# Issuing the scatters of three sequences one at a time between the steps of a recurrent stage (attention, routed experts and a dense block on one Trainium2 core)

## Chip, cores and metric

The kernel runs on one core of one Trainium2 chip. The metric is the device time of one execution in microseconds (us). Three runs of the kernel before gave 576.25, 574.99 and 574.95 us, so its time is the median, 574.99 us.

## What is computed

Three parts follow one another. A gated linear recurrence over 4 sequences (b) of 768 tokens with 8 heads gives 3072 rows of 384 values. A router then sends part of the rows to one of 8 experts each, and a dense block with a maximum over three products makes the output.

```python
for t in range(S):                                    # recurrence, per b and head
    state = alpha[:, :, t, :, None] * state + einsum('bhd,bhe->bhde', k[:, :, t], v[:, :, t])
    y[:, :, t] = einsum('bhd,bhde->bhe', q[:, :, t], state)
...
do_compute = x @ w_skip > 0                           # routed experts
e_idx = argmax(xc @ w_gate)
y[mask] = gate_w[mask, None] * (maximum(xc[mask] @ w1[e], 0.0) @ w2[e])
out[do_compute] = xc + y
...
h = maximum(maximum(x @ w1, x @ w2), x @ w3)          # dense block
return h @ w_out
```

## The kernel before

**Chunks.** The recurrence is cut into 24 chunks of 128 tokens, 6 for each sequence; chunk n = 6b + c is the n-th turn of the loop `for n, (b, c) in enumerate(seq)`. In turn n TensorE (PE) does, in this order: `scores(n+1)` (L284, keys by queries), `trans(n+1)` (L275), `rows(n-1)` (L330, the output of the chunk before, turned to token rows), `outs(n)` (L317 with the running state, L320 with the masked scores), and `upd(n)` (L302, the state's update). In this document chunk n begins where the first L320 product of chunk n starts.

**Around PE.** VectorE (DVE) makes two scans for chunk n+3 (L241, L255), two masks of the scores of chunk n+1 (L290), and adds the old state to the new (L305, reads PE's L302). ScalarE (ACT) copies out of the accumulators: `yt` (L323, reads PE's L317 and L320 and feeds L330), the rows `xr` (L349), and the scaled state `ws` (L307, reads DVE's L305 and feeds L317 of the next chunk). GpSimd (POOL) multiplies the keys and the queries by the scans' results: `k` at L244 and `q` at L259, one each a chunk, for chunk n+3; PE needs them two turns later.

**Router and scatters.** When the six chunks of a sequence are through, its 768 rows are given slots. For sequences 0 and 1 the generator `early` does this, for sequences 2 and 3 the generator `route` (sequence 3 in two parts of 4 and 2 chunks). A generator yields between its steps, and `step_routes()`, called twice a turn (after `outs` and at the turn's end), takes it one step on. `route` finds the expert of each row (`om`, L460), counts (`ec`, L462), asks PE for the ranks in two small products (`pr`, L471 and L472, which read `om` and `ec`), and works out the slot numbers `si` (L476 to L485). Then POOL scatters the rows: six indirect DMAs a sequence (L415), each of 128 rows of 386 values (384 values, a weight, the token's number) to the table `slots` in DRAM. In `scatter` the pace is set by yields:

```python
if b == B - 2 and 0 < c < NC - 1:      # sequence 2: one scatter a step
    yield 1
elif b < B - 2 and c % 2 and c < NC - 1:   # sequences 0, 1: two, then one turn on
    yield 1
    yield 1
```

POOL itself takes its queue in order and starts a scatter as soon as `si` and the rows are there. After turn 20 there are no more `k` and `q` to make, so nothing stands between the six scatters of sequence 2 in POOL's queue.

**After the chunks.** In turn 22 the queue of SP loads the first 256 rows of `slots` back (`xe`, L619), which waits for the scatters of sequences 0 to 2; PE reads `xe` at L642 after chunk 23. The six scatters of sequence 3 come after that. Then the experts begin (first product at L756), and from there PE is busy to the end.

Of the kernel before, what the change touches and what calls it, by code (L numbers as in the profile page):

```python
# [83 lines left out]
def tile_gla_moe_moe2(ctx, tc, akq, vp, wgt, cst, io, ew, md, out):  # L84
# [41 lines left out]
    with tc.manual_schedule():  # L126
# [135 lines left out]
        def prep(j):  # L262
            if j < nseq:
                sf = suffixes(j)
                inverse(j, sf)
                prefixes(j, sf)
# [88 lines left out]
            return low_part  # L355

        nroute = [0]
        scat = []
        ecs = []

        def early(b, c0, c1):
            om = wk.tile([128, NE, NC + 1], BF16, name=f"om{NC}")
            ec = wk.tile([128, NE, NC + 1], BF16, name=f"ec{NC}")
            r = lambda nm, w, dt=F32: wk.tile([128, NC, w], dt, name=nm)
            mx, md, sm, ra, s1, dl, rk = (r(*z) for z in (
                ("mx", 1), ("md", 1), ("sme", 1), ("ra", 1), ("s1", 1), ("dl", NE), ("rk", NE)))
            s2, mi = (cols[nm][:, 0:NC, None] for nm in ("s2", "mi"))
            t = cols["t"].rearrange("p (c e) -> p c e", c=NC)
            si, lh, ls_, tr_ = r("si", 1, I32), r("lh", 18), r("lgs", NE + 1), r("tr", 6)
            ex, xb, l8 = exs[b % 2], xr[b], ls_[:, :, 0:NE]  # L370
            bc = lambda a: a.to_broadcast([128, NC, NE])
            ce = lambda a: a.rearrange("p e c -> p c e")
            fl = lambda a: a.rearrange("p e c -> p (e c)")
            h = lx[b].rearrange("p c a e -> p c (a e)")
            nroute[0] += 1
            A.copy(om[:, :, 0:1], ecs[-1] if ecs else cnt[:, :, None])
            G.tensor_tensor(lh, h[:, :, 0:18], h[:, :, 18:36], ALU.add)
            G.tensor_tensor(ls_, lh[:, :, 0:9], lh[:, :, 9:18], ALU.add)
            SY.dma_start(out=x2[b * S:(b + 1) * S, :].rearrange("(c p) d -> p c d", p=128), in_=xb[:, :, 0:DM])
            yield 1  # L380
            V.tensor_reduce(mx, l8, AX.X, ALU.max)
            G.tensor_tensor(dl, l8, bc(mx), ALU.subtract)
            yield 1
            yield 1
            V.scalar_tensor_tensor(t, dl, 0.0, cols["rev"][:, None, :].to_broadcast([128, NC, NE]), ALU.is_equal, ALU.mult)
            V.tensor_reduce(mi, t, AX.X, ALU.max)
            V.scalar_tensor_tensor(md, ls_[:, :, NE:NE + 1], 0.0, mi, ALU.is_le, ALU.add)
            A.activation(ex[:, :, 0:NE], dl, AF.Exp)
            yield 1
            V.tensor_tensor(ce(om)[:, 1:], t, bc(md), ALU.is_equal)  # L390
            V.tensor_tensor_scan(fl(ec), cols[NC].bitcast(BF16), fl(om), 0.0, ALU.mult, ALU.add)
            ecs.append(ec[:, :, NC:NC + 1])
            yield 1
            pr = ps_r.tile([128, NE, NC], F32, name="pr")
            T.matmul(pr, ltri, om[:, :, 1:], start=True, stop=False)
            T.matmul(pr, ones, ec[:, :, 0:NC], start=False, stop=True)
            G.tensor_tensor(tr_[:, :, 0:4], ex[:, :, 0:4], ex[:, :, 4:8], ALU.add)
            G.tensor_tensor(tr_[:, :, 4:6], tr_[:, :, 0:2], tr_[:, :, 2:4], ALU.add)
            G.tensor_tensor(sm, tr_[:, :, 4:5], tr_[:, :, 5:6], ALU.add)
            G.tensor_tensor(sm, sm, ex[:, :, NE:], ALU.add)  # L400
            yield 1
            V.tensor_tensor(rk, ce(pr), ce(om)[:, 1:], ALU.mult)
            V.tensor_reduce(ra, rk, AX.X, ALU.add)
            V.scalar_tensor_tensor(s1, mi, -float(CAP), ra, ALU.mult, ALU.add)
            A.copy(xb[:, :, DM + 1:DM + 2], tokid[:, b * NC:(b + 1) * NC, None])
            yield 1
            V.reciprocal(xb[:, :, DM:DM + 1], sm)
            V.tensor_scalar(s2, ra, float(CAP - OFF), 8192.0, ALU.is_ge, ALU.mult)
            V.scalar_tensor_tensor(si, s2, float(OFF + NSLOT), s1, ALU.add, ALU.add)
            yield 1  # L410
            yield from scatter(b, 0, NC, si)

        def scatter(b, c0, c1, si):
            for c in range(c0, c1):
                i_ = G.indirect_dma_start(  # L415
                    out=slots, out_offset=bass.IndirectOffsetOnAxis(ap=si[:, c - c0, :].bitcast(U32), axis=0),
                    in_=xr[b][:, c, :], in_offset=None, bounds_check=NSLOT - 1, oob_is_err=False)
                for j_ in scat:
                    tc.declare_no_dep(i_.ins, j_.ins, reason="every row of every scatter has a slot of its own")
                scat.append(i_)  # L420
                if b == B - 2 and 0 < c < NC - 1:
                    yield 1
                elif b < B - 2 and c % 2 and c < NC - 1:
                    yield 1
                    yield 1
            yield 1

        def route(b, c0, c1):
            n = c1 - c0
# [36 lines left out]
                         in_=xb[:, :, 0:DM])  # L466
            yield 1
            if not last:
                yield 1
            pr = ps_r.tile([128, NE, n], F32, name="pr")  # L470
            T.matmul(pr, ltri, om[:, :, 1:], start=True, stop=False)  # L471
            T.matmul(pr, ones, ec[:, :, 0:n], start=False, stop=True)  # L472
# [13 lines left out]
            def onehot():  # L486
                for c in range(n):
                    V.tensor_scalar(p0[:, c0 + c], iota[:, 0:CAP], s2[:, c], None, ALU.is_equal)
                    yield 1 if c0 + c == 0 else 0
                yield 1  # L490

            if last:
                if c0:
                    A.copy(cnt, ec[:, :, n])
                yield from onehot()
                V.tensor_scalar(si[:, 0:n], s2, 0.0, None, ALU.add)
            V.tensor_reduce(sm, ex, AX.X, ALU.add)
            V.reciprocal(xb[:, :, DM:DM + 1], sm)
            A.copy(xb[:, :, DM + 1:DM + 2], tokid[:, b * NC + c0:b * NC + c1, None])
            yield from scatter(b, c0, c1, si)  # L500

        rw, wr = {}, {}

# [35 lines left out]
        def step_routes():  # L539
            for r in reversed(routes):  # L540
                stage(r)
# [19 lines left out]
        for n, (b, c) in enumerate(seq):  # L561
            if n + 1 < nseq:
                scores(n + 1)
                trans(n + 1)
            if n < 2:
                prep(n + 2)
            elif n == 2:
                prefixes(4, half)
            else:
                prep(n + 3)  # L570
            if n + 1 < nseq:
                mask(n + 1, 0)
                mask(n + 1, 1)
            if n == 1:
                half = first_half(4)
            if n == 2:
                prep(5)
            low_part = rows(n - 1) if n else None
            if n == nseq - 2:
                A.copy(xq[0][:, 0:2], xr[B - 1][:, 0:2, 0:DM])  # L580
                rA = route(B - 1, 0, 4)
            if n > nseq - 3:
                stage(rA)
            outs(n)
            step_routes()
            upd(n)
            if n > nseq - 3:
                stage(rA)
            if n == nseq - 1:
                xlow(0)  # L590
            if n > nseq - 4:
                low_part()
            if n == 0:
                vload(4)
            vload(n + 5)
            if n and seq[n - 1][1] == NC - 1:
                routes.append((early if b < B - 1 else route)(b - 1, 0, NC))
            step_routes()
            if n == 3:
                V.tensor_copy(cols["rev"], rev)  # L600
            if n == 10:
                SY.dma_start(out=iota, in_=io)
            if 3 <= n < 7:
                for i in range((n - 3) * NSLOT // 512, (n - 2) * NSLOT // 512):
                    SY.dma_start(out=slots[i * 128:(i + 1) * 128, :], in_=zt)
            if 7 <= n < 11:
                wpart(n - 7)
            if n in (13, 14, 15, 19):
                wsplit(min(n - 13, 3), G)
            if n in (17, 20):  # L610
                wload((n - 14) // 3)
            if n == nseq - 4:
                rs.close()
                xep = xes.enter_context(tc.tile_pool(name="xep", bufs=1, side="right"))
                xq += [xep.tile([128, NC, DM], F32R, name=f"xq{i}") for i in range(2)]
                p0 = xep.tile([128, NC, CAP], F32R, name="p0")
                xe = xep.tile([128, 2, DM], F32, name="xe")
            if n == nseq - 2:
                SY.dma_start(out=xe, in_=slots[0:CAP, 0:DM].rearrange("(m p) d -> p m d", p=128))  # L619
# [848 lines left out]
```

## Time and profile before

| | before |
|---|---|
| median of three runs | 574.99 us |
| the profiled execution: its own time | 575.13 us |
| the profiled execution: span from first to last instruction | 573.3 us |
| PE busy in the span | 562.1 us (98%) |
| DVE, ACT, POOL busy in the span | 408.8, 300.5, 257.7 us |
| granted clock of PE, mean over the span | 0.994 |
| scatters at L415 | 24, busy 23.7 us |

The profiled execution's own time is 1.8 us above its span, which is the work around the program, and 0.14 us above the median of the runs. The page gives busy time by engine and by slice of the span; the timelines give each instruction's start, length, and the time that its engine sat idle before it, with what ended the wait. A busy share is a mean over stages with different limits: what an edit of the scatters is worth stands in the stretch of the chunks (about the first 140 us) and in the waits there.

### The profile page before, as it was taken

Reading aid. Unit: us, or ns where it says so; the run is one execution under the profiler, and the core shown is the slowest. Engines: PE = TensorE matmul, PEld = TensorE weight load, DVE = VectorE, ACT = ScalarE, POOL = GpSimd, SP = SyncE. Lnnn points to the kernel's source line nnn. Section 1 sums busy time; section 2 is a strip of 40 time slices with the busy share of each in tenths; the row PEclk is TensorE's granted clock in tenths of the full one; section 3 lists DMA queues with packets and bytes.
Section 4 is the critical chain, followed back from the end, with each engine's and each line's share of the span. In section 5 each row is a group of like instructions: output and inputs, shape, how many; then the busy total and the mean of one; then the engine's idle time right before and its main releaser. Section 6 shows DMA issues by size and latency. Waiting matters only on the chain. (4 is left out here: it accounts for less than half of the span.)

```text
span 573.3 us, 11006 instructions
## 1 busy us (share of the span) xinstructions
PE 562.1 (98%) x4149; PEld 502.8 (88%) x4149; DVE 408.8 (71%) x697; ACT 300.5 (52%) x654; POOL 257.7 (45%) x216
## 2 busy tenths in 40 slices
PE   7999999979999999999999999999999999999997
PEld 4999888969999999999988888888788899787896
DVE  8998979927677767777589995694667584766700
ACT  4666676634667676667343445454544474455311
POOL 6654789843366555756222022112554501456320
PEclk9999999979999999999999999999999999999999
DMA  8899997743668988895328159335654624556011
GB/s 324 315 297 337 377 363 247 279 154 141 208 245 306 319 308 293 269 306 207 116 100 284 37 186 365 137 125 177 219 196 151 223 96 145 186 195 217 2 57 59
DMA packets 51150, 122.79 MB, mean 214 GB/s; under 512 B 4594, under 2 KB 38752, under 8 KB 47504
## 3 DMA queue, kind: packets, MB, share of 16 engines
q1 hardware_dynamic: 47856, 116.19, 58.7%
q0 software_dynamic: 2560, 4.83, 2.2%
q10 hardware_dynamic: 672, 0.98, 0.6%
q8 instruction: 34, 0.56, 0.4%
q14 instruction: 28, 0.23, 0.1%
HBM read 92.76 MB, written 32.28 MB: 218 GB/s over the span
## 5 line engine op out<-in xcount | busy, mean ns | idle before, releaser
L124 POOL TENSOR_TENSOR wl<-raw,wh 128x768 fp32r<-128x768 f32 x26 | 53.7, 2064 | 32.8 <-ACT wh L123 31.9
L123 ACT CAST wh<-raw 128x768 fp32r<-128x768 f32 x64 | 53.5, 837 | 14.6 <-PE po L776 13.9
L756 PE MATMUL ph<-xh,wh 128*128 128x256 f32 x192 | 56.4, 294 | 0.0
L757 PE MATMUL ph<-xl,wh 128*128 128x256 f32 x192 | 54.4, 283 | 0.1
L758 PE MATMUL ph<-xh,wl 128*128 128x256 f32 x192 | 54.4, 283 | 0.0
L776 PE MATMUL po<-wh,hl 128*128 128x384 f32 x128 | 43.2, 337 | 0.0
L775 PE MATMUL po<-wl,hh 128*128 128x384 f32 x128 | 43.1, 337 | 0.0
L774 PE MATMUL po<-wh,hh 128*128 128x384 f32 x128 | 42.9, 335 | 0.0
L124 DVE TENSOR_TENSOR wl<-raw,wh 128x768 fp32r<-128x768 f32 x38 | 36.4, 958 | 9.0 <-ACT wh L123 8.4
L762 DVE SCALAR_TENSOR_TENSOR hl<-ph,hh 128x256 fp32r<-128x256 f32 x64 | 26.8, 419 | 16.5 <-ACT hh L761 15.2
L244 POOL TENSOR_TENSOR k<-akq,sf 128x512 f32<-128x512 f32 x24 | 28.4, 1185 | 19.7 <-DVE sf L241 12.3
L757 PEld LDWEIGHTS ph<-xl,wh 128*128 128x128 f32 x192 | 36.4, 190 | 0.5 <-issue 0.3
L756 PEld LDWEIGHTS ph<-xh,wh 128*128 128x128 f32 x192 | 36.5, 190 | 0.2 <-ACT xh L123 0.2
L758 PEld LDWEIGHTS ph<-xh,wl 128*128 128x128 f32 x192 | 36.3, 189 | 0.0
L415 POOL DMA_INDIRECT slots<-xr,si x24 | 23.7, 987 | 23.8 <-DVE s L482 15.5
L761 ACT ACTIVATE hh<-ph 128x256 fp32r<-128x256 f32 x64 | 24.7, 385 | 16.2 <-PE ph L758 12.7
L284 PE MATMUL ps<-q,k 64*128 64x128 f32 x384 | 30.0, 286 | 2.2 <-POOL q L259 1.8
L255 DVE TENSOR_TENSOR_SCAN ap<-akq,pcs 128x521 f32<-128x521 f32 x24 | 29.8, 1241 | 1.8
L259 POOL TENSOR_TENSOR q<-akq,ap 128x512 f32<-128x512 f32 x24 | 28.4, 1183 | 5.6 <-DVE ap L255 5.6
L241 DVE TENSOR_TENSOR_SCAN sf<-akq,pcs 128x520 f32<-128x520 f32 x24 | 29.5, 1228 | 1.5 <-DMA akq<-in_akq_dram 1.3
L290 DVE TENSOR_TENSOR sm<-ps,cs 128x512 f32<-128x512 f32 x48 | 30.3, 673 | 0.0
L1141 POOL TENSOR_TENSOR tb<-tb,tb 128x512 f32<-128x512 f32 x12 | 15.5, 1293 | 31.5 <-ACT tb L1140 31.5
(683 smaller groups left out, 1734.2 us busy)
## 6 DMA issues: line engine op xcount, KB each, us to landing
raw<-in_ew_dram SPq DMA_DIRECT2D x15, 1536.0 KB
akq<-in_akq_dram SPq DMA_DIRECT2D x21, 772.5 KB
rm<-in_md_dram SPq DMA_DIRECT2D x12, 768.0 KB
mh<-wd SPq DMA_DIRECT2D x7, 1024.0 KB
ml<-wd SPq DMA_DIRECT2D x7, 896.0 KB
raw<-wd SPq DMA_DIRECT2D x6, 1024.0 KB
raw<-wd SPq DMA_DIRECT2D x6, 896.0 KB
vt<-in_vp_dram SPq DMA_DIRECT2D x24, 200.0 KB
```

The costliest lines, as they stand in the source:

```text
L123: A.copy(h, src)
L124: (eng or V).tensor_tensor(l, src, h.bitcast(F32), ALU.subtract)
L241: V.tensor_tensor_scan(sf[:, KW - 2::-1], al[:, KW - 1:0:-1], eb[:, KW - 1:0:-1], 0.0, ALU.mult, ALU.max)
L255: V.tensor_tensor_scan(ap, al, eb, 0.0, ALU.mult, ALU.max)
L284: T.matmul(ps[i][:, p, :], kh[j][r0:r0 + 64, p, :], qh[j][r0:r0 + 64, p, :], start=True, stop=True)
L290: V.tensor_tensor(t, fr[j][i], cmask[:, None, :].to_broadcast([128, NP, C]), ALU.mult)
L756: T.matmul(ph, wh[:, z], xh_[e][:, k, :], start=(k == 0), stop=False)
L757: T.matmul(ph, wh[:, z], xl_[e][:, k, :], start=False, stop=False)
L758: T.matmul(ph, wl[:, z], xh_[e][:, k, :], start=False, stop=(k == k3 - 1))
L774: T.matmul(po, hh[:, zm], wh, start=(f == 0), stop=False)
L775: T.matmul(po, hh[:, zm], wl, start=False, stop=False)
L776: T.matmul(po, hl[:, zm], wh, start=False, stop=(f == nf1 - 1))
```

## The change

The pace of the scatters is no longer set by yields in `scatter`. `early` and `route` put their six scatters into a list (`pend_sc`), and `scatter_next()` takes one from it at fixed places: in turns 3 to 19 between `k` and `q` of chunk n+3 and at the turn's end; in turn 20 after `k` and at the end; from turn 21 on after `rows(n-1)` and at the end. For sequence 2 the scatters of chunks 2 to 5 each follow a copy of the token's numbers on ACT (`late`), which POOL has to wait for; the copy stood before as one for all six chunks. To have `si` earlier, `route` of sequence 2 also takes its steps sooner: the weight (L497, L498) moves ahead, the ranks `pr` go to PE at the end of turn 19 and no longer within turn 20, and the slot numbers are made ahead of the masks in turn 20. Sequence 3 is scattered as before.

```diff
--- before.py
+++ after.py
@@ -408,22 +408,23 @@
             V.scalar_tensor_tensor(si, s2, float(OFF + NSLOT), s1, ALU.add, ALU.add)
             yield 1
-            yield from scatter(b, 0, NC, si)
-
-        def scatter(b, c0, c1, si):
-            for c in range(c0, c1):
...
-                if b == B - 2 and 0 < c < NC - 1:
-                    yield 1
-                elif b < B - 2 and c % 2 and c < NC - 1:
-                    yield 1
-                    yield 1
+            pend_sc.extend((b, c, si, False) for c in range(NC))
             yield 1
+
+        def scatter(b, c, si, late):
+            if late:
+                A.copy(xr[b][:, c, DM + 1:DM + 2], tokid[:, b * NC + c:b * NC + c + 1])
+            i_ = G.indirect_dma_start(
...
+        def scatter_next():
+            if pend_sc:
+                b, c, si, late = pend_sc.pop(0)
+                scatter(b, c, si[:, c, :], late)
@@ -466,7 +467,9 @@
             yield 1
             if not last:
-                yield 1
+                V.tensor_reduce(sm, ex, AX.X, ALU.add)
+                V.reciprocal(xb[:, :, DM:DM + 1], sm)
+                A.copy(xb[:, 0:2, DM + 1:DM + 2], tokid[:, b * NC:b * NC + 2, None])
             pr = ps_r.tile([128, NE, n], F32, name="pr")
@@ -489,15 +492,20 @@
-            if last:
-                if c0:
-                    A.copy(cnt, ec[:, :, n])
...
+            if not last:
+                pend_sc.extend((b, c, si, c > 1) for c in range(NC))
+                yield 1
+                return
...
-            yield from scatter(b, c0, c1, si)
+            for c in range(n):
+                scatter(b, c0 + c, si[:, c, :], False)
+            yield 1
@@ -566,16 +574,28 @@
-            else:
-                prep(n + 3)
+            elif n + 3 < nseq:
+                half = suffixes(n + 3)
+                if n + 4 < nseq:
+                    scatter_next()
+                inverse(n + 3, half)
+                if n + 4 < nseq:
+                    prefixes(n + 3, half)
+                else:
+                    step_routes()
+                    scatter_next()
             if n + 1 < nseq:
                 mask(n + 1, 0)
                 mask(n + 1, 1)
+            if n + 4 == nseq:
+                prefixes(n + 3, half)
...
             low_part = rows(n - 1) if n else None
+            if n + 3 >= nseq:
+                scatter_next()
@@ -596,6 +616,7 @@
             step_routes()
+            scatter_next()
```

On POOL the six scatters of sequence 1 and of sequence 2 stand as follows (`xr_818` is the row tile of sequence 1, `xr_1309` of sequence 2, `xr_1801` of sequence 3); before:

```order
L415 DMA slots_64<-xr_818,si_1256 2048x386 x2
L244 TENSOR_TENSOR k2_1697<-akq1_170,sf_1694 128x512
L259 TENSOR_TENSOR q2_1704<-akq1_170,ap_1700 128x512
L415 DMA slots_64<-xr_818,si_1256 2048x386 x2
L244 TENSOR_TENSOR k2_1783<-akq2_171,sf_1780 128x512
L259 TENSOR_TENSOR q2_1790<-akq2_171,ap_1786 128x512
L124 TENSOR_TENSOR wl_1841<-raw_859,wh_1840 128x768
L244 TENSOR_TENSOR k2_1864<-akq3_172,sf_1861 128x512
L259 TENSOR_TENSOR q2_1871<-akq3_172,ap_1867 128x512
L415 DMA slots_64<-xr_1309,si_1926 2048x386 x6
L415 DMA slots_64<-xr_1801,si_2135 2048x386 x4
```

and with the change:

```order
L417 DMA slots_64<-xr_818,si_1256 2048x386
L259 TENSOR_TENSOR q2_1704<-akq1_170,ap_1700 128x512
L417 DMA slots_64<-xr_818,si_1256 2048x386
L244 TENSOR_TENSOR k2_1780<-akq2_171,sf_1777 128x512
L417 DMA slots_64<-xr_818,si_1256 2048x386
L259 TENSOR_TENSOR q2_1790<-akq2_171,ap_1786 128x512
L124 TENSOR_TENSOR wl_1847<-raw_859,wh_1846 128x768
L244 TENSOR_TENSOR k2_1870<-akq3_172,sf_1867 128x512
L417 DMA slots_64<-xr_1309,si_1879 2048x386
L259 TENSOR_TENSOR q2_1892<-akq3_172,ap_1888 128x512
L417 DMA slots_64<-xr_1309,si_1879 2048x386 x5
L417 DMA slots_64<-xr_1801,si_2139 2048x386 x4
```

The scatters of sequence 1 stand alternately with `k` and `q` where they stood in pairs; of sequence 2 one stands ahead of the last `q`, and the other five follow it with nothing between them on POOL's own queue.

On ACT the copies of the token's numbers (`xr<-cs`) that the scatters of sequence 2 wait for stand so in turns 20 to 22; before:

```order
L307 ACTIVATE ws_139<-pu,totm 128x48 x4
L499 COPY xr<-cs 128x6
L277 COPY kk<-pk 128x512
L348 CAST xq_1945<-px 128x384
L349 COPY xr<-px 128x384
L323 COPY yt<-py 128x512
L307 ACTIVATE ws_138<-pu,totm 128x48 x4
```

and with the change:

```order
L307 ACTIVATE ws_139<-pu,totm 128x48 x4
L277 COPY kk<-pk 128x512
L348 CAST xq_1945<-px 128x384
L349 COPY xr<-px 128x384
L416 COPY xr<-cs 128x1
L323 COPY yt<-py 128x512
L307 ACTIVATE ws_138<-pu,totm 128x48 x4
L416 COPY xr<-cs 128x1
```

One copy for six chunks has become one copy ahead of each of four scatters (two of the four stand in these rows), half a turn apart; a copy for the first two chunks stands earlier, in turn 19.

On PE the ranks of sequence 2 (`pr`; `om` and `ec` come from DVE) stand in turn 20 before:

```order
L320 MATMUL py<-sm_1794,vt 64x128
L471 LDWEIGHTS ltri
L471 MATMUL pr<-om_1748,ltri 128x48
L472 LDWEIGHTS ones
L472 MATMUL pr<-ec_1749,ones 128x48
L302 MATMUL pu<-vt,kk 64x48 x8
```

and with the change at the end of turn 19:

```order
L320 MATMUL py<-sm_1708,vt 64x128
L302 MATMUL pu<-vt,kk 64x48 x8
L474 LDWEIGHTS ltri
L474 MATMUL pr<-om_1748,ltri 128x48
L475 LDWEIGHTS ones
L475 MATMUL pr<-ec_1749,ones 128x48
L284 MATMUL ps_1850<-q_1704,k_1694 128x128
```

They stood between L320 and L302 of chunk 20; now the scores of the next chunk stand right behind them in PE's queue.

## Rows read from the trace of the kernel before

**Rows 1.** Stretches, one chunk each, and three others: length, busy time, clock, DMA.
```profile
core 0: us, PE busy (x) PEld busy (x) DVE busy (x) ACT busy (x) POOL busy (x), PEclk, DMA share, GB/s
51.41:56.46 5.05, 5.05 (x79) 4.60 (x77) 4.57 (x11) 3.46 (x13) 2.10 (x2) 1.00 1.08 342
...
56.46:61.42 4.96, 4.96 (x76) 4.29 (x74) 4.11 (x10) 2.49 (x11) 2.82 (x6) 1.00 1.02 310
...
105.06:110.28 5.22, 5.22 (x78) 4.78 (x76) 5.01 (x11) 3.53 (x10) 4.29 (x5) 1.00 0.82 307
110.28:115.64 5.36, 5.36 (x80) 4.70 (x78) 4.04 (x14) 3.65 (x12) 4.09 (x4) 1.00 0.67 230
115.64:126.16 10.52, 6.77 (x74) 5.44 (x72) 2.91 (x9) 3.06 (x11) 4.93 (x6) 0.85 0.26 98
126.16:131.46 5.30, 5.30 (x61) 5.00 (x59) 2.48 (x13) 2.33 (x9) 0.00 (x0) 0.65 0.71 223
...
139.80:145.00 5.20, 5.13 (x38) 4.93 (x38) 2.46 (x5) 1.92 (x6) 3.89 (x5) 1.00 0.30 107
...
124.30:129.70 5.40, 5.40 (x52) 4.98 (x52) 2.75 (x11) 2.82 (x10) 0.00 (x0) 0.50 0.63 191
```

**Rows 2.** POOL's timeline: start, length (us), line, operation, idle before and its end.
```profile
105.44 0.97 POOL L415 DMA_INDIRECT slots<-xr,si  x1 [0.30 <-issue]
...
112.29 1.17 POOL L259 TENSOR_TENSOR q<-akq,ap 128x512 f32<-128x512 f32 x1
114.72 1.01 POOL L415 DMA_INDIRECT slots<-xr,si  x1 [1.26 <-issue]
...
121.13 0.97 POOL L415 DMA_INDIRECT slots<-xr,si  x1 [0.30 <-issue]
```

**Rows 3.** PE's timeline, the products of chunks 19 to 22 and L642.
```profile
105.06 1.10 PE L320 MATMUL py<-sm,vt 128*64 128x128 f32 x16
...
106.54 1.34 PE L284 MATMUL ps<-q,k 64*128 64x128 f32 x16
...
110.28 1.09 PE L320 MATMUL py<-sm,vt 128*64 128x128 f32 x16
...
115.64 1.09 PE L320 MATMUL py<-sm,vt 128*64 128x128 f32 x16
116.57 0.62 PE L302 MATMUL pu<-vt,kk 128*64 128x48 f32 x16
...
124.26 1.97 PE L317 MATMUL py<-q,ws 64*64 64x128 f32 x16 [2.18 <-ACT ws L307]
126.16 1.97 PE L320 MATMUL py<-sm,vt 128*64 128x128 f32 x16
...
136.50 0.69 PE L642 MATMUL pk<-cs,xe 128*128 128x128 f32 x4
```

**Rows 4.** ACT's timeline, the copies out of chunks 19, 20, 21, and the state.
```profile
107.03 0.59 ACT L323 COPY yt<-py 128x512 f32<-128x512 f32 x1 [1.61 <-PE pu L302]
...
111.42 0.59 ACT L323 COPY yt<-py 128x512 f32<-128x512 f32 x1 [0.47 <-PE py L320]
...
118.96 0.59 ACT L323 COPY yt<-py 128x512 f32<-128x512 f32 x1 [3.30 <-PE ps L284]
123.72 0.88 ACT L307 ACTIVATE ws<-pu,totm 128x48 f32<-128x48 f32 x4 [4.17 <-DVE pu L305]
```

**Rows 5.** DVE's timeline, the counts of sequence 2 and the state of chunk 21.
```profile
107.13 0.27 DVE L462 TENSOR_TENSOR_SCAN ec<-pcs,om 128x56 bf16<-128x56 bf16 x1
...
123.31 0.37 DVE L305 TENSOR_TENSOR pu<-pu,ws 128x192 f32<-128x192 f32 x1 [7.42 <-PE px L330]
```

**Rows 6.** Sum over the five stretches 61.42:66.87, 75.49:80.88, 91.07:96.30, 99.88:105.06, 105.06:110.28.
```profile
sum 26.47, PE 26.42 PEld 23.87 DVE 23.31 ACT 17.44 POOL 22.22; mean PE 5.28 PEld 4.77 DVE 4.66 ACT 3.49 POOL 4.44
```

**Rows 7.** SP's queue, the load of xe.
```profile
125.85 0.45 SPq L619 DMA_DIRECT2D xe<-slots  x1
```

**Rows 8.** The line view of L415: shortest, median, longest in ns, first and last start.
```profile
L415 POOL DMA_INDIRECT slots<-xr,si x24: 967/970/1164, 64.5 to 143.9; - x24
```

More of the change, by code (lines that the diff above doesn't have):

```diff
@@ L357, in tile_gla_moe_moe2 @@
         nroute = [0]
-        scat = []
+        scat, pend_sc = [], []
         ecs = []
@@ L410, in early @@
             yield 1
-            yield from scatter(b, 0, NC, si)
-        def scatter(b, c0, c1, si):
-            for c in range(c0, c1):
[L415 to L420, printed above, removed]
-                if b == B - 2 and 0 < c < NC - 1:
-                    yield 1
-                elif b < B - 2 and c % 2 and c < NC - 1:
-                    yield 1
-                    yield 1
-            yield 1
+            pend_sc.extend((b, c, si, False) for c in range(NC))
+            yield 1
+        def scatter(b, c, si, late):
+            if late:
+                A.copy(xr[b][:, c, DM + 1:DM + 2], tokid[:, b * NC + c:b * NC + c + 1])
+            i_ = G.indirect_dma_start(
+                out=slots, out_offset=bass.IndirectOffsetOnAxis(ap=si.bitcast(U32), axis=0),
+                in_=xr[b][:, c, :], in_offset=None, bounds_check=NSLOT - 1, oob_is_err=False)
+            for j_ in scat:
+                tc.declare_no_dep(i_.ins, j_.ins, reason="every row of every scatter has a slot of its own")
+            scat.append(i_)
+        def scatter_next():
+            if pend_sc:
+                b, c, si, late = pend_sc.pop(0)
+                scatter(b, c, si[:, c, :], late)
         def route(b, c0, c1):
@@ L490, in onehot @@
                 yield 1
-            if last:
-                if c0:
-                    A.copy(cnt, ec[:, :, n])
-                yield from onehot()
-                V.tensor_scalar(si[:, 0:n], s2, 0.0, None, ALU.add)
+            if not last:
+                pend_sc.extend((b, c, si, c > 1) for c in range(NC))
+                yield 1
+                return
+            if c0:
+                A.copy(cnt, ec[:, :, n])
+            yield from onehot()
+            V.tensor_scalar(si[:, 0:n], s2, 0.0, None, ALU.add)
             V.tensor_reduce(sm, ex, AX.X, ALU.add)
```

## Prediction

> **What bounds the kernel now.** The page comes first: PE is busy in 98% of the span, so a gain can lie only where PE idles, is held up, or runs at a lower clock. The stretches are next, cut where the L320 products of a chunk start [rows 1]. A chunk without scatters takes 5.05 us with PE busy throughout, and 4.96 us where the next chunk needs no transpose: this is PE's own pace. One chunk falls out: chunk 21 takes 10.52 us with PE busy for 6.77 of them, and chunk 22 takes 5.30 us at a mean granted clock of 0.65. In the middle of that, from 124.30 to 129.70 us, the granted clock is 0.50, the 1.2 GHz level; PE had been mostly waiting for the 6 us before.
>
> What sits in that hole is read from POOL's timeline [rows 2]: six scatters of sequence 2, one after another without a break, from 114.72 to 122.10 us (the first and the last stand in the rows, 0.30 us between neighbours). PE's timeline [rows 3] shows that L302 of chunk 21 was over at 116.57 + 0.62 = 117.19 us, and DVE's that the addition which reads it started at 123.31 us, after 7.42 us of idling [rows 5]; the scaled state came at 123.72 [rows 4] and L317 of chunk 22 only at 124.26 us [rows 3]. So DVE had its operands, had nothing else to do, and still waited until 1.2 us after the last scatter. The copy `yt` measures this three times [rows 4] against the end of the L320 products that it waits for [rows 3]: with no scatter about (chunk 20) it starts 111.42 − 111.37 = 0.05 us after them, beside a pair of scatters (chunk 19; the second runs to 106.41 [rows 2]) 107.03 − 106.16 = 0.87 us, beside the six 118.96 − 116.73 = 2.23 us. I read this so: while scatters are issued, word from one engine to another comes late, and in an unbroken run of them it piles up. That is an inference from three waits, not something a row states.
>
> **The change part by part.** Durations are those of the profiled execution, so the sum starts from its 575.13 us (0.14 above the median of the runs).
>
> *The run of six is broken up.* The change makes five of the six wait for something on ACT or DVE, or for their place behind `q`. One goes ahead of the last `q`, one behind it, four behind copies half a turn apart on ACT, so some 2 us apart on average, and words can pass between them. Chunk 21 then falls back to PE's pace, 10.52 − 4.96 = **5.56 us** gained; chunk 20 loses its surplus, 5.36 − 5.05 = **0.31 us**. Chunk 22 gets the full clock: its L320 products take 1.97 us at half clock against 1.09 us [rows 3], 0.88 us on the path, and half of the L330 products behind them adds some 0.2: **1.1 us**.
>
> *The ranks go to PE a turn earlier.* They now stand ahead of the scores of chunk 21, which started at 106.54 us [rows 3], and wait for `ec`, which ends at 107.13 + 0.27 = 107.40 us [rows 5]. PE has nothing to put in the gap, so it loses 0.86 us and about 0.1 for the start; if the last scatter of sequence 1, which now stands behind `k` and so beside this very wait, delays it by the 0.87 us seen beside a pair, 1.8 us. I take **−1.3 us**, between. The products themselves cost the same in either place.
>
> *Six single scatters beside chunks 20 to 23.* Not shown before. Low end nothing; far end what the run costs, 5.56 us, which is a rival below. The nearest rows are the five chunks with pairs, 26.47 us in sum [rows 6], so 26.47 − 5 × 5.05 = 1.2 us for five pairs, 0.24 us a pair. These chunks have less work to hide a late word behind than the earlier ones, so I take most of a pair's price for each single: **−1.2 us** (0 to −2.4).
>
> *Twelve single scatters of sequences 0 and 1.* Their number, length and order among `k` and `q` stay; `q` has the same work ahead of it and `k` one scatter less. Best, the 1.2 us of the pairs vanish; worst, each single costs 0.24, which is 12 × 0.24 − 1.2 = 1.7 us lost. I take **+0.6 us**.
>
> *DVE and ACT.* Weight and slot numbers move ahead of the last scan and the masks in turn 20. The masks of chunk 21 come some 1 us later; their scores are ready at 106.54 + 1.34 = 107.88 us and the L320 products that read them start at 115.64 us [rows 3], time enough for both. The last `q` ended at 112.29 + 1.17 = 113.46 us [rows 2] for scores that follow L302 at 117.19; with one scatter (0.97) and the later scan ahead of it, it ends some 1.5 us later and still in time. Four small copies on ACT replace one: they sit beside ACT's idling (it is busy for 3.06 of 10.52 us in chunk 21 [rows 1]). Without that cover each would cost less than the 0.59 us of a `yt` copy [rows 4].
>
> *The load of xe.* It waits for the last scatter of sequence 2, whose copy now stands behind the state of chunk 22. From the end of L302 of that chunk (T): the addition 0.37 [rows 5], the state 0.88 [rows 4], copy and starts, so a scatter at T + 1.9; in the trace the load was issued 125.85 − 121.13 = 4.7 us after the last scatter's start [rows 7, 2], part of it behind another store, so I put it at 2.5 to 4.7 later. Its 0.39 MB at the 223 GB/s of that stretch [rows 1] take 1.8 us: ready at T + 6.2 to 8.4. PE wants it at 136.50 us, 8.4 us after the L320 products of chunk 22 end [rows 3]; less 0.62 for L302 and some 0.6 for the clock, that is T + 7.1. So nothing to 1.3 us; I take **−0.3 us**.
>
> Sum: 5.56 + 0.31 + 1.1 − 1.3 − 1.2 + 0.6 − 0.3 = 4.8 us. The experts start that much earlier and PE is busy from there to the end, so nothing should take it back: 575.13 − 4.8 = **570.4 us**.
>
> **The rivals.**
>
> *The hole is not made by the scatters* (chance 0.08). Something that falls at the same time makes it, and it stays. For it speaks that six scatters in a row, up to 143.9 us [rows 8], run beside the first expert's products, and PE is busy for 5.13 of 5.20 us there [rows 1]. Against it: those products wait for little that is fresh, while every wait in chunk 21 is for a result just made; and DVE's wait ended just after the last scatter. The time would be 575.13 + 1.3 − 0.6 = 575.8 us.
>
> *Each single costs as much as a burst* (slower; chance 0.06). Then it is not the run but the number of separate issues that counts, 18 now. Of the sum 5.56 + 0.31 + 1.1 + 1.2 (the pairs' price) − 1.3 − 0.3 = 6.6 us remains to be eaten by 18 × h; the kernel is slower by over 0.3% (1.7 us) from h = 8.3 / 18 = 0.46 us on. The pairs' 0.24 us speaks against it, the 5.56 / 6 = 0.93 us in the run for it. With h = 0.6 us: 575.13 − 6.6 + 10.8 = 579.3 us.
>
> *The tail gives part back* (chance 0.08): scatters bunch behind the copies, the last ones land late, and `xe` or the singles take 2 us more than I put: 572.5 us.
>
> *DVE shuts POOL out* (chance 0.02). In the rows a scatter takes 967 to 1164 ns over all 24 [rows 8], with DVE busy 5.01 of 5.22 us beside some of them [rows 1]; no scatter waits for DVE there. As a mechanism here: each of the six scatters would wait for the DVE instruction in progress, on average 5.01 / 11 = 0.46 us [rows 1], and pass that on: 6 × 0.46 = 2.7 us, 573.1 us. The Trainium skill (SBUF — State Buffer, SBUF: two separate sides) has the rule for this: descriptors that GpSimd generates cannot be written while a VectorE instruction holds the port that the two share, and a transfer of about 620 ns took about 3100 ns that way. By that figure, taken for six scatters, an estimate, some 15 us of POOL time would be added. The trace does not bear the rule out for these instructions.
>
> **How the numbers follow.** Chances: the forecast 0.76, and 0.08, 0.06, 0.08, 0.02 for the rivals. About 0.3% (1.7 us) is what a measurement of this kernel can tell from no change. Faster by more: the forecast but for its slow end, the tail and the port, 0.84. Same: the first rival and a little of the others, 0.09. Slower: 0.07. The range: the best ends give 4.8 + (1.3 − 0.95) + 1.2 + 0.6 + 0.3 = 7.3 us gained, 567.9; the poor ends 4.8 − 0.5 − 1.2 − 1.0 = 2.1 us gained, 573.0. It is stretched a little for the tail: 567.4 to 573.6 us.
>
> **What would show it.** Right: chunk 21 at about 5 us, a granted clock of 1.00 throughout chunks 21 to 23, DVE's L305 of chunk 21 within 1 us of L302, six separate scatters on POOL, and a gap of about 1 us before the scores of chunk 21. Wrong: a hole of several us still in chunks 20 to 22, `xe` awaited by L642, or chunks 10 to 20 longer than before.

## The result, and the profile after

| us | before | after |
|---|---|---|
| median of 5 runs each, on one chip (the first pair) | 575.62 (574.95 to 576.25) | 569.86 (569.42 to 570.10) |
| the profiled execution: its own time | 575.13 | 570.10 |
| the profiled execution: span | 573.3 | 568.3 |
| granted clock of PE, mean over the span | 0.994 | 1.000 |

The ratio after to before is 0.9899, with a 95% interval from 0.9889 to 0.9910. The forecast was 570.4 us, 567.4 to 573.6. So the forecast held for this pair. The runs below add something that the pair could not show: **on chips 0 and 1 the kernel before itself takes 568 us, and on chip 1, where the change was run too, it gains nothing.**

In the code after, the scatter stands at L417, `ec` at L463, `pr` at L474 and L475, the load of `xe` at L640, its products at L663, the copies of the token's numbers at L416. The stretches of chunks 19 to 22 (PE, PEld, DVE, ACT and POOL busy, granted clock, DMA share, GB/s) now are:

```profile
105.36:111.44 6.08, 5.42 (x81) 4.79 (x79) 5.50 (x17) 3.84 (x13) 4.63 (x4) 1.00 0.68 253
111.44:116.49 5.05, 5.05 (x79) 4.60 (x77) 3.66 (x7) 2.99 (x10) 4.70 (x5) 1.00 0.71 248
116.49:121.20 4.71, 4.71 (x75) 4.26 (x73) 2.25 (x6) 2.55 (x12) 2.03 (x3) 1.00 0.36 137
121.20:125.92 4.72, 3.67 (x60) 3.34 (x59) 3.13 (x16) 3.24 (x12) 1.96 (x3) 1.00 0.59 210
```

Beside [rows 1] the reader sees chunk 21 at 4.71 us for 10.52, with PE busy throughout; chunk 22 at 4.72 for 5.30 and at full clock; chunk 20 at 5.05 for 5.36; and chunk 19 at 6.08 for 5.22, where PE now idles. POOL's timeline of the same stretch, against [rows 2]:

```profile
113.19 1.01 POOL L417 DMA_INDIRECT slots<-xr,si  x1 [0.16 <-issue]
...
115.59 1.01 POOL L417 DMA_INDIRECT slots<-xr,si  x1 [0.17 <-issue]
116.90 0.97 POOL L417 DMA_INDIRECT slots<-xr,si  x1 [0.30 <-ACT xr L416]
120.25 0.97 POOL L417 DMA_INDIRECT slots<-xr,si  x1 [2.38 <-ACT xr L416]
121.52 0.97 POOL L417 DMA_INDIRECT slots<-xr,si  x1 [0.30 <-ACT xr L416]
124.95 0.97 POOL L417 DMA_INDIRECT slots<-xr,si  x1 [2.45 <-ACT xr L416]
```

They are not six singles but one, a pair, a pair and one: the copies that a scatter waits for (its gate, below) hold two of them back only in name, because POOL was still at the scatter before (the 0.30 us is what lies between any two neighbours). Three lines of PE's timeline show the two waits that the change leaves, and that `xe` is not awaited (no bracket on the last line):

```profile
107.44 0.19 PE L474 MATMUL pr<-om,ltri 128*128 128x48 bf16 x1 [0.54 <-issue]
...
123.79 1.14 PE L330 MATMUL px<-rps,yt 128*128 128x105 f32 x8 [1.05 <-ACT yt L323]
...
130.97 0.69 PE L663 MATMUL pk<-cs,xe 128*128 128x128 f32 x4
```

**Where the 5 us came from.** Cut chunk by chunk at the first L320 product, after against before: chunks 10 to 18 gave 0.37 us in sum, chunk 19 cost 0.86, chunk 20 gave 0.31, chunk 21 5.81, chunk 22 0.56 (these from starts of 0.01 us, so 5.29 for the 5.30 in the rows). That is 6.19 us. Chunk 0 started 0.66 us later in this execution, before anything that the change touches; over all fourteen traces it starts between 11.90 and 12.99 us whatever the kernel. So the first expert product comes 5.54 us earlier (139.80 to 134.26 us), and chunk 23 as much; 0.5 us of it is lost again by the end, 0.1 in the later stages and 0.4 behind the last product, and 5.0 us of span remain.

### The profile page after: what moved, and what is told of

It is laid out like the page before. It is cut to its first block, busy times and chain, and to the rows that moved or that the text cites. A ratio compares the mean times of both kernels' runs of the same rounds, so it can differ in the third digit from the quotient of the medians.

```text
span 568.3 us, 11013 instructions
## 1 busy us (share of the span) xinstructions
PE 557.4 (98%) x4149; PEld 499.4 (88%) x4149; DVE 409.2 (72%) x697; ACT 301.3 (53%) x658; POOL 258.7 (46%) x216
## 5 line engine op out<-in xcount | busy, mean ns | idle before, releaser
L124 POOL TENSOR_TENSOR wl<-raw,wh 128x768 fp32r<-128x768 f32 x26 | 53.7, 2066 | 32.7 <-ACT wh L123 30.7
L124 DVE TENSOR_TENSOR wl<-raw,wh 128x768 fp32r<-128x768 f32 x38 | 36.5, 960 | 9.1 <-ACT wh L123 8.5
L417 POOL DMA_INDIRECT slots<-xr,si x24 | 24.1, 1003 | 16.5 <-DVE s L485 6.1
```

The lines of the kernel that those rows point to most:

```text
L124: (eng or V).tensor_tensor(l, src, h.bitcast(F32), ALU.subtract)
```

## The experiments

Twelve runs, e1 to e12, were made on three chips, and each occasion also timed the kernel before beside them:

| chip | the kernel before there, median | kernels run |
|---|---|---|
| of the first pair (not recorded) | 575.62 (5 runs) | before, after |
| 0 | 568.34 (567.65 to 569.15, 21 runs) | e1 to e4 |
| 1 | 567.89 (567.33 to 569.07, 27 runs) | e5 to e7 |
| 1, a second time | 568.08 (567.50 to 568.96, 13 runs) | e8, e9 |
| 2 | 575.64 (575.14 to 576.13, 13 runs) | e10 to e12 |

Below, the chips on which the kernel before takes 568 us are called quiet. A chip and an occasion cannot be told apart by these runs: chip 1 was quiet on two occasions, chips 0 and 2 were used on one each.

The theories at the start: **A**, an unbroken run of scatters holds back word between the engines and so makes the hole; **B**, the hole comes from the order of ranks, slot numbers and masks, which the change also moved; **C**, something else that falls at 117 to 123 us makes it. On the way **D** was added: the hole needs a condition that some occasions have and others don't. A "notice" below is an engine's increment of a semaphore that another engine waits on.

**e1: one row of five.** The gates go (the copies on ACT that four of the scatters wait for): one copy for all six rows, and five scatters stand in a row behind the last `q`.

```diff
-                A.copy(xb[:, 0:2, DM + 1:DM + 2], tokid[:, b * NC:b * NC + 2, None])
+                A.copy(xb[:, 0:NC, DM + 1:DM + 2], tokid[:, b * NC:b * NC + NC, None])
-                pend_sc.extend((b, c, si, c > 1) for c in range(NC))
+                pend_sc.extend((b, c, si, False) for c in range(NC))
```

> The changed kernel with one part undone: the scatters of sequence 2 wait for no copies (the numbers of all six chunks are copied in turn 19), so five of them follow the last q on POOL without a break; the earlier ranks and slot numbers stay. Theory A (an unbroken run makes the hole): chunk 21 takes 9 to 11 us again, the granted clock falls to 0.50 for some us behind it, DVE's L305 of chunk 21 starts several us after L302 ends; time 574.5 to 576.5 us, about that of the kernel before. Theory B (the gain came from the order of ranks, slot numbers and masks): chunk 21 stays at 4.7 us, time 569.5 to 570.5 us.

Measured: 569.08 us (567.96 to 569.77, 10 runs), 1.0011 of before (1.0002 to 1.0020). Chunk 21 took 4.66 and chunk 22 3.97 us, with five scatters in a row beside them. No hole, and none in the kernel before either, whose time of 568.34 us leaves no room for it.

**e2: all six in turn 22,** behind one copy, where no `k` or `q` is left.

```diff
+            if n == nseq - 2:
+                A.copy(xr[B - 2][:, :, DM + 1:DM + 2], tokid[:, (B - 2) * NC:(B - 1) * NC, None])
+                for _ in range(NC):
+                    scatter_next()
```

> The changed kernel with all six scatters of sequence 2 behind one copy of the token numbers in turn 22, one after another. Theory A: the hole moves along: chunk 21 takes 4.7 us, chunk 22 grows from 4.72 us by 3 to 6 us, and the load of xe comes later and is awaited by PE at its products before the experts; time 574 to 578 us. Theory C (something else at 117 to 123 us made the hole): chunks 21 and 22 as in the changed kernel but for up to 3 us of waiting for xe; time 570 to 573 us.

Measured: 576.14 us (one run). The loss looks like a hole moved, and is none. Its stretches (chunk 22, then 130 to 140 us) and one line of PE's timeline:

```profile
120.52:124.49 3.97, 3.68 (x61) 3.35 (x59) 3.14 (x16) 3.19 (x11) 2.95 (x3) 1.00 0.69 249
130.00:135.00 5.00, 0.36 (x1) 0.37 (x2) 2.01 (x10) 0.00 (x0) 0.00 (x0) 0.80 0.63 186
135.00:140.00 5.00, 5.00 (x25) 4.95 (x24) 0.29 (x1) 0.64 (x2) 3.71 (x4) 0.52 0.49 193
```
```profile
134.63 1.22 PE L664 MATMUL pk<-cs,xe 128*128 128x128 f32 x4 [4.95 <-DMA xe<-slots]
```

Chunk 22 runs at full pace beside the first three of the six, which start at 120.84 us and follow each other without a break. What is late is `xe`: the last scatter ends at 128.35 us, the load goes out at 130.84, PE stands for 4.95 us and then works at a granted clock of 0.52. So the deadline that the prediction counted for `xe` is real, and missing it costs about as much as the hole. The Trainium skill (Perfetto Trace Analysis, DMA Instruction — SWDGE (GPSIMD)) says that such an instruction's bar ends when its descriptors are made, not when the data have moved. The runs fit this: a scatter is on POOL for 0.97 us, and the median from its issue to its landing was 3.9 us in e1.

**e3: two rows of three,** the second behind one copy.

> The changed kernel with the scatters of sequence 2 in two runs of three, behind the last q and behind one copy at the end of turn 21. Theory A, with a price that grows faster than the run's length (a pair 0.24 us, six 5.6 us): three cost 0.5 to 2 us each, so chunks 21 and 22 together take 10.5 to 13 us against 9.43 us in the changed kernel; time 570.5 to 573.5 us. If the price went by number alone (0.93 us each): the two chunks take as much as with single scatters, 9.4 us, time 570 us.

Measured: 569.03 us (one run); chunks 20 to 22 took 5.05, 4.66 and 3.97 us. It tells nothing that e1 did not.

**e4: the ranks behind the next scores,** scatters as in the change.

```diff
+                yield 1
             pr = ps_r.tile([128, NE, n], F32, name="pr")
...
                 scores(n + 1)
                 trans(n + 1)
+            if n + 4 == nseq:
+                step_routes()
```

> The changed kernel with the ranks of sequence 2 given to PE behind the scores and the transposes of turn 20, not at the end of turn 19. If PE's wait for the counts is what makes chunk 19 take 6.08 us: chunk 19 falls to 5.1 to 5.3 us, chunk 20 stays at 5.05 to 5.2 us, the single scatters start where they did, and the time is 0.7 to 0.9 us under the changed kernel, 569.0 us. If the wait only moves (slot numbers late, the last scatter and xe late): chunk 20 or the products on xe take it back, 569.9 us.

Measured: 568.47 us (567.54 to 569.06, 11 runs), 1.0000 of before (0.9991 to 1.0009). Chunk 19 took 5.30 us, where e1 to e3 and the change have 6.08 or 6.09, so the ranks' place costs some 0.8 us of chunk 19. For B this says nothing, since no hole was there to bring back.

After these four, A had fallen in its plain form: five or six scatters in a row are not enough.

**e5 and e6: the two kernels, word for word,** profiled on chip 1.

> The kernel before, word for word, profiled beside the one after. The four runs already made fell against theory A (any unbroken run of scatters makes the hole): a run of five took 4.66 us in chunk 21 and a run of six 3.97 us in chunk 22, with no matrix or vector engine late. Theory D: the hole needs a condition that was there when the first pair of traces was taken (there, some thirty notices of engines to each other between 65 and 146 us land 0.3 to 4.7 us late, in both kernels) and is not here (one or two such in each of the four runs). D expects the time near 568.3 us, chunk 21 near 4.7 us, chunks 20 to 22 near 5.3, 4.7 and 4.0 us, clock 1.00 there, and few late notices. Theory A', that only the run of six in its old place (its first scatter at 114.7 us, behind the last query multiplication) makes the hole, expects chunk 21 near 10.5 us and a time near 575.5 us.

> The changed kernel, word for word, on the same chip as the kernel before. D: about 5 us from the hole are gone on both sides, so the change is left with what it does itself: ranks 0.86 us later in chunk 19, the gates in chunk 22 0.7 us, less 0.3 to 0.7 us from scatters taken singly; near 568.5 to 569.5 us, ratio 1.000 to 1.002 to before. A': 569.9 us as in the first pair, with before at 575.5, ratio 0.990.

Measured: before 567.9 us (567.36 to 568.57, 11 runs), after 568.41 (568.03 to 569.05, 11 runs), 1.0008 of before (0.9999 to 1.0017). Chunks 20 to 22 of the kernel before on this chip, and DVE's addition that in [rows 5] started at 123.31 us:

```profile
110.08:115.44 5.36, 5.36 (x80) 4.70 (x78) 4.08 (x14) 3.69 (x12) 4.16 (x4) 1.00 0.68 235
115.44:120.10 4.66, 4.66 (x75) 4.21 (x73) 2.34 (x6) 2.40 (x9) 3.44 (x5) 1.00 0.43 166
120.10:124.07 3.97, 3.68 (x61) 3.35 (x60) 3.13 (x16) 3.09 (x10) 1.51 (x2) 1.00 0.73 259
```
```profile
117.03 0.37 DVE L305 TENSOR_TENSOR pu<-pu,ws 128x192 f32<-128x192 f32 x1 [1.33 <-PE pu L302]
```

The six scatters stand where they stood, from 114.52 to 121.92 us at the same 0.97 to 1.01 us each, and DVE starts 0.05 us after L302 (which ends at 116.36 + 0.62 us) in place of 6.1. Same program, same place, no hole. That is D.

**e7: five in a row and the ranks behind the scores** (the edits of e1 and e4).

> Two edits of the changed kernel together: the ranks go to TensorE behind the next scores and transposes (as in the run that took 5.30 us in chunk 19 for 6.08), and the scatters of the third sequence without gates, five in a row (as in the run whose chunk 22 took 3.97 us for 4.73). D: chunk 19 5.30, chunk 21 4.66, chunk 22 3.97 us, so 1.5 us under the changed kernel on this chip and within 0.5 us of the kernel before: near 568.0 us. A': the same, as five in a row made no hole, and then 7 us under the kernel before.

Measured: 568.01 us (567.26 to 568.88, 11 runs), 1.0001 of before (0.9992 to 1.0010), as D said. The other theory named there (A') expected the same time, so e7 does not part the two; e5 has done that.

**e8 (e1 once more) and e9 (the kernel before with twelve scatters).** In e9 each scatter of sequence 2 is issued a second time into a spare table, so the run is of twelve.

> The changed kernel with its third sequence's scatters in one row of five, once more, to see both kernels' times on a further occasion. Theory D (the hole belongs to an occasion, not to the program): either this occasion is like the last two, the kernel before near 568 us, this one within 0.3% of it, chunk 21 4.66 us; or it is like the first pair, the kernel before near 575.5 us, and then this one holds a row of five of its own and late notices with it: chunk 21 or 22 some 2 to 5 us long, 571 to 575 us. A' (only the run of six in its old place makes it): 568 to 570 us on every occasion.

> The kernel before with every scatter of the third sequence issued a second time, into a spare buffer: the run is of twelve, about 15.4 us of GpSimd instead of 7.7, and twice the rows written. If scatters in a row hold back the other engines' notices in proportion (theory A in a weaker form: the six are just under a limit here), the count of late notices rises from one or two and chunks 21 to 23 go over 4.7, 4.0 and 4 us by a microsecond or more each. D: chunk 21 stays at 4.66 and chunk 22 at 3.97 us with clock 1.00; the last scatter ends near 130 us, 7.7 us later, so the load of the slots waits for it, and TensorE stands about 4 to 6 us before the products of that load: near 573 us, all of it from that wait.

Measured: e8 568.86 us (568.46 to 569.11, 10 runs), 1.0011 of before (1.0001 to 1.0021). e9 574.53 (574.31 to 575.52, 4 runs), 1.0115 (1.0098 to 1.0131). In e9 chunk 21 took 4.66 and chunk 22 3.97 us at full clock, beside twelve scatters without a break, and the whole loss is PE's 4.80 us before the products of `xe`, with the lower clock behind it (0.56 from 134.04 to 139 us). In these two chunks the length of the run costs the other engines nothing on this chip.

**e10 to e12: chip 2, where the hole is back.** e10 is the kernel before, e11 is e4 (scatters gated) and e12 is e7 (five in a row); e11 and e12 differ in the gates alone.

> The kernel before once more, to see whether the hole comes back. D (it belongs to an occasion): either 568 us with chunk 21 at 4.66 us, as on the last three occasions, or 575.5 us with chunk 21 near 10.5 us; nothing between. A' (it belongs to the program) has already fallen and would want 575.5.

> Scatters singly with their gates, ranks behind the next scores. On an occasion like the last three: 568 to 568.5 us, chunk 19 5.30, chunk 21 4.66, chunk 22 3.97 us. On one like the first pair: near 569 us, 0.8 us under the changed kernel there (chunk 19 5.3 for 6.08), chunk 21 4.7, chunk 22 4.7.

> Five scatters in a row, ranks behind the next scores. On an occasion like the last three: 568.0 us, level with the kernel before (1.0001 there). On one like the first pair this tells whether five in a row are held up as six were: yes, chunk 21 or 22 longer by 2 to 5 us and 571 to 574 us; no, 568 to 569 us.

| chip 2 | time, us | to before (95%) | chunk 20 | chunk 21 | chunk 22 |
|---|---|---|---|---|---|
| e10, run of six | 575.09 (574.91 to 576.03, 10 runs) | 0.9995 (0.9985 to 1.0004) | 5.36 | 10.51 | 4.67 |
| e12, run of five | 572.99 (572.62 to 573.12, 4 runs) | 0.9954 (0.9937 to 0.9970) | 5.26 | 7.38 | 5.19 |
| e11, gated | 569.59 (569.40 to 569.67, 4 runs) | 0.9895 (0.9879 to 0.9912) | 5.24 | 4.65 | 5.27 |

Chunk 21 in e10, in the view of stretches, and the start of DVE's addition in its timeline:

```profile
115.77:126.28 10.51, 6.96 (x74) 5.60 (x72) 2.90 (x9) 3.05 (x11) 4.95 (x6) 0.75 0.23 86
```
```profile
123.44 0.37 DVE L305 TENSOR_TENSOR pu<-pu,ws 128x192 f32<-128x192 f32 x1 [7.41 <-PE px L330]
```

The same two views of e12:

```profile
115.73:123.11 7.38, 4.81 (x75) 4.29 (x73) 1.46 (x4) 2.18 (x8) 4.58 (x5) 1.00 0.44 169
```
```profile
121.14 0.37 DVE L305 TENSOR_TENSOR pu<-pu,ws 128x192 f32<-128x192 f32 x1 [4.76 <-remote]
```

And of e11:

```profile
115.29:119.94 4.65, 4.65 (x74) 4.20 (x72) 2.23 (x5) 2.73 (x12) 2.08 (x3) 1.00 0.47 183
```
```profile
117.89 0.37 DVE L305 TENSOR_TENSOR pu<-pu,ws 128x192 f32<-128x192 f32 x1 [1.96 <-PE pu L302]
```

L302 of chunk 21 ended at 117.32, 117.28 and 116.83 us in the three, so the same addition waited 6.1, 3.9 and 1.1 us for it. With everything but the gates equal, five scatters in a row cost 7.38 − 4.65 = 2.7 us in chunk 21 (3.4 us in the time, the start of chunk 0 0.44 us later included), and chunk 22 is long in both, in e12 because the granted clock there is 0.67, in e11 because PE waits 1.59 us at full clock for `yt`. The six in a row of e10 stand 10.51 − 4.65 = 5.9 us above e11 in chunk 21; e10 also differs from e11 in the places of ranks, slot numbers and masks, and how much of the 5.9 is theirs was not separated. The pair that the gates leave beside chunk 22 costs 5.27 − 3.97 = 1.3 us, if the quiet chips are the measure. On such a chip A holds for a row of five, and B and C are not needed for that.

**What tells the two kinds of chip apart in a trace.** Of the 2041 to 2047 increments that the engines' instructions make, those whose semaphore shows no event within 0.25 us of the instruction's end were counted over the whole span. They are 49 and 52 in the first pair and 57 to 60 in e10 to e12, all but three of each between 60 and 147 us, where the 24 scatters stand; in the nine runs on chips 0 and 1 there are 1 to 3. With gates (e11) the count is no smaller than without (e12). What the gates change is how late: of those between 113 and 125 us, the one that waited longest for the next event of its semaphore waited 4.7 us in the kernel before, 4.6 in e10 and 5.6 in e12, but 1.2 us in the changed kernel and 1.6 in e11.

What a chip or an occasion must have for this was not found. No run here changes it, so the cause of the lateness itself stays open. Every run on record carries a span and a granted clock, so none shows whether the lateness is there when nothing is recorded.

## Why the prediction was right, and where not

- **The run of six: right in mechanism and size for the chip of the pair, wrong as a rule.** Chunk 21 gave 5.81 us for the forecast 5.56; its pace without late word is 4.66 us and not 4.96, since the chunk that the 4.96 was read from also holds two rank products (L395, L396) and chunk 21 holds none. e12 against e11 shows for chip 2 the cause that the prediction inferred from three waits; for the chip of the pair that is argued, from the same chunk, the same late addition and a like count of late increments. But the sentence "while scatters are issued, word from one engine to another comes late" holds on the chip of the first pair and on chip 2 and fails on chips 0 and 1, even with twelve in a row (e9). The prediction took one profile for the program's own behaviour.
- **Chunk 20:** 0.31 us forecast, 0.31 measured. Chip 1 shows the same, 5.36 to 5.05, so this part is not from late word. The two rank products left this chunk. In chunk 9 they cost 4.96 − 4.66 = 0.30 us, so the 0.31 is most likely theirs and belongs against the term of the ranks; that the number fits is luck.
- **Clock and singles in chunks 21 and 22:** +1.1 and −1.2 forecast, together −0.1; measured +0.56 in chunk 22. The clock came as forecast (1.00 for 0.65). The singles were priced too high for the pair: 4.73 − 3.97 = 0.76 us in chunk 22 and 0.05 in chunk 21, if the quiet chips are the measure, for 1.2. On chip 2 they cost more, 5.24 − 5.05 = 0.19 us in chunk 20 and 1.30 in chunk 22 (e11).
- **The price of a pair, 0.24 us, was misread,** and both terms on singles rest on it. The prediction took 5.05 us as the pace of the five chunks of [rows 6]. The same five chunks of the kernel before on chip 1 (e5: 61.66:67.10, 75.72:80.77, 90.79:96.16, 99.73:104.91, 104.91:110.08), with the same pairs beside them and almost no late word, are as long but for 26.47 − 26.21 = 0.26 us, 0.05 us a pair:

```profile
sum 26.21, PE 26.21 PEld 23.83 DVE 24.13 ACT 18.49 POOL 21.97; mean PE 5.24 PEld 4.77 DVE 4.83 ACT 3.70 POOL 4.39
```

- **Ranks:** −1.3 forecast, −0.86 measured, and 6.08 or 6.09 us in chunk 19 on every chip with this order. The wait was 0.54 us, for 0.86 forecast, and the two products the rest, which chunk 20 gives back. The prediction counted the wait to the end of `ec`; the first product reads `om` alone, and in e6, where its wait is 0.55 us, the bracket names `om`. The late-word surcharge (1.8 at worst) did not come. e4 shows that the loss is not needed.
- **Twelve singles of sequences 0 and 1:** +0.6 forecast, +0.37 measured (chunks 10 to 18).
- **xe:** −0.3 forecast, 0 measured. The load went out at 127.41 us and PE took its rows at 130.97 without a wait. e2 and e9 show what lies behind that edge: 4.95 and 4.80 us.
- **The signs named ahead:** chunk 21 near 5 us (4.71), clock 1.00, and DVE's L305 within 1 us of L302 (0.59 us: 118.62, in the line below, against 117.41 + 0.62) came; the gap before the scores was 0.5 us of waiting, not 1; six separate scatters were two singles and two pairs.

```profile
118.62 0.37 DVE L305 TENSOR_TENSOR pu<-pu,ws 128x192 f32<-128x192 f32 x1 [1.87 <-PE pu L302]
```

- **What was not in the sum:** the start, 0.66 us later by chance, and 0.5 us lost behind the experts' start. The misses nearly cancel: 6.2 us gained in the chunks, 5.0 in the end, 4.8 forecast. That the forecast time came within 0.3 us of the profiled one is in part luck.
- **The rivals.** "The hole is not made by the scatters" falls by e11 and e12 on one chip, though e1 to e9 seemed to bear it out: there a run of scatters made no hole. "Each single costs as much as a burst" falls: 0.8 us for all six is 0.14 us each in the pair, and 1.5 us are 0.25 each on chip 2, against the 0.46 from which it decides. "The tail gives part back" did not come. "DVE shuts POOL out" falls for the hole and for the change by this line of the changed kernel (shortest, median, longest in ns; first and last start):

```profile
L417 POOL DMA_INDIRECT slots<-xr,si x24: 969/1012/1165, 65.1 to 138.4; - x24
```

24 scatters, now singly beside a busy DVE, take 1165 ns at the longest, as in [rows 8]. But it does not fall altogether. In four runs on the quiet chips (e3, e4, e5, e7) one scatter of the 24, the last of sequence 3, takes 1.76 us. In e5 it runs from 136.56 to 138.32 us, and a subtraction of DVE on 768 values a row (L124) runs from 136.53 to 137.47: DVE was 0.03 us ahead, and the scatter ended 0.85 us after it. This looks like the wait that the Trainium skill (SBUF — State Buffer, SBUF: two separate sides) describes, where descriptors of GpSimd cannot be written until VectorE releases the port that the two share; no run here tests it. The scatter stands behind the chunks, beside the first expert's products.

## What to carry to other kernels

Time a change on more than one chip and occasion before its gain is believed: here the same two programs differ by 1% on the chip of the pair and by nothing on chip 1, and only a trace from each showed where the difference lies. Keeping indirect scatters apart, so that other engines' word can pass between them, cost nothing measurable on the quiet chips (e4: 1.0000 of before) and saved 1% on chip 2, where e11 is the same kernel, as long as the last one still lands before its reader. Whether e4 (e11) beats the change is not shown: e11 is at 0.9895 of before on chip 2, the change, which was not run there, at 0.9899 on the chip of the first pair, and the intervals cover each other.

## What the runs showed of the hardware that was not expected

- Chips or occasions differ: the same kernel before takes 575.1 to 575.6 us on two occasions and 567.9 to 568.3 on three, each with a spread under 2 us. Most of the difference lies in chunk 21 (10.51 against 4.66 us) and in chunk 22 at the lower clock behind it (4.67 or 5.29 against 3.97); some tenths lie in earlier chunks beside scatters.
- Where it happens, a scatter itself is no longer (medians of 0.97 us in e5 and e10); what is late is the end of other engines' waits. The same wait of DVE ended 6.1 us after its operand beside six scatters in a row, 3.9 beside five, 1.1 beside a pair, and 0.05 us on a quiet chip beside six.
- The lower clock came behind PE's waiting with either cause: in e2, after 4.95 us of waiting for a load, the granted clock is 0.52 from 135 to 140 us, near the level of 1.2 GHz, as it was 0.50 behind the hole in [rows 1]. In e12, where PE waited 2.57 us in chunk 21, the clock of chunk 22 was 0.67.
